# A long convolution over a period of 23040 in place of 25088: 91 frequencies along n1 in place of 99

## The chip, the cores and the metric

The kernel runs on one core of one Trainium2 chip. The metric is the device time of one execution in microseconds (us). A core has five engines that work side by side: PE (TensorE, matrix products), DVE (VectorE), ACT (ScalarE), POOL (GpSimd) and SP (SyncE, which here only issues DMAs). They meet at semaphores. Operands lie in the on-chip memory SBUF; PE writes into PSUM only.

## The reference

```python
S, D = 12480, 128                                # x, v: (1, S, D)
h = np.maximum(pos_emb @ w1, 0.0) @ w2           # (S, 64) -> (S, 64) -> (S, D)
h = h * np.exp(-0.01 * np.arange(S, dtype=np.float32))[:, None]
u = x * v
L = 2 * S
y = np.fft.irfft(np.fft.rfft(u, n=L, axis=1) * np.fft.rfft(h, n=L, axis=0)[None], n=L, axis=1)[:, :S]
x1 = (x * y)[0]                                  # (S, D)
a = x1 @ moe_w_in                                # (S, 2048)
x2 = (a * np.clip(a + 3.0, 0.0, 6.0) / 6.0) @ moe_w_out
b = x2 @ moe2_w_in
out = np.where(b > 0.0, b, np.exp(np.minimum(b, 0.0)) - 1.0) @ moe2_w_out
```

A causal convolution of each of 128 channels with a filter as long as the sequence, a product with x, and two gated layers with 2048 hidden columns. All in float32; the four large weight matrices arrive as float64 bit patterns. The convolution need not be taken over 2S points: any period will do at which the wrapped part of the full result falls outside the first S outputs, or is zero.

## The kernel before

**Transform.** The period is L = N1 x N2 = 196 x 128 = 25088. Position n is split as n1 x 128 + n2. Of the N1 rows only H1 = 98 hold data, and because the data are real NK = 99 frequencies k1 (0 to 98) are kept. The stages:

- *Filter* (`filter_hidden`): the hidden layer of the filter in 8 pieces, with the decay window.
- *First transform* (`first`, L308): for every n2, over n1, for 4 channels at a time: 8 matmuls, each with 2 x NK columns of the table `t1`. Done for the channels of u (`first_u`, into `au`) and for the hidden filter columns (`first_r`, into `Ar`). ACT copies the result out of PSUM (L311). `au` lies as [channel, k1, re/im], so one channel's row is 2 x NK floats.
- *Signals* (`signal`, L264 to L267): POOL multiplies x by v for 4 channels and folds the halves (three operations, on 98 partitions). There are 16 per half of the channels. They don't depend on NK.
- *Second transform* (`second_all`): for every k1, over n2, with one 128 x 128 table `gm` per k1. The k1 go in *groups* of 4 (`KGROUPS`), the last groups are smaller. In half 0 of the channels PE transforms the filter rows too (`second_r`, L333, copied back by ACT at L336), then the signal (`second_u`, L325) and the filter's output layer (`second_h`, L340) into one PSUM tile `z`. Then the complex product (`second`): ACT copies the filter part to `ta` (L345), DVE makes two products `tb` and `tc` (L347), POOL adds and subtracts them into `au` (L353, two operations a group). In half 0 two groups, A and B, go together: a *pair*. Half 1 takes the groups one by one and doesn't transform the filter again.
- *Middle*: between the two halves, `first_u` of half 1 (L308) alternates with the *third transform* (`third`, L362) of half 0, over 128 columns of `cs`; DVE combines the results (L368).
- *Third transform* of half 1, then the *fourth* (L479, over k1, 97 or 98 columns), the product with x (L525), and the two gated layers (L594 and L638), each split into high and low parts.

**Weights.** The float64 weights are converted beside the convolution. `weight_steps` is a generator with 32 conversions of three steps:

- step 1: DVE L180, L181;
- step 2: ACT L184, L185 (these need L180), DVE L186, and DMAs: one store of the conversion before (L170, from ACT's queue) and one load (L165, from SP's);
- step 3: DVE L190 (needs L185), L191.

**Order.** Each engine executes in program order. `convert(n)` adds n to `due` and takes as many steps as are due. It is called behind every first transform of the first stage (rate `RATE[0]`), behind every group of half 0 (`RATE[1]`), every chunk of the middle (`RATE[2]`) and every group of half 1 (`RATE[3]`); in the halves only for groups with k0 below `KLAST`. The call stands at the end of a group, so its DVE and ACT operations stand ahead of the next group's copies and products:

```python
            for z, gm, k0, nk in g:
                if not early:
                    second_h(hf, z, k0, nk)
                second(hf, z, k0, nk)
                if hf == 0:
                    load_gm0(n + len(gms))
                n += 1
                convert(RATE[2 * hf + 1] if k0 < KLAST else 0)
```

PSUM holds four tiles of the pool `ps`. The table pieces of half 0 go through eight buffers (`gms`), those of half 1 through four (`ld`). `AHEAD` places two signals of half 1 between groups of half 0, `TAIL` marks where the filter rows of the last groups are transformed in one go. All loads are issued by SP in program order.

Of the kernel before, what the change touches and what calls it, by code (L numbers as in the profile page):

```python
# [16 lines left out]
PSUM = bass.MemoryType.PSUM  # L17

S, D, FO, FF = 12480, 128, 64, 2048
N1, N2 = 196, 128  # L20
L = N1 * N2
H1 = N1 // 2
NK = H1 + 1
HN = N2 // 2
NM = HN + 1
SP = H1 * N2
HP = H1 * HN
HD = D // 2
SHIFT = H1 // 4
TT = 512  # L30
# [6 lines left out]
LAG, DELAY = 5, 13  # L37
EX = 8
SIG = (16, 40)
KLAST = 72  # L40

# [1 line left out]
TOKENS = {  # L45
    (m, sg): (np.arange(H1) * N2 + m - 1 if sg else np.arange(H1 - 2, -1, -1) * N2 + N2 - 1 - m) for m, sg in CLASSES
}
# [4 lines left out]
def tables():  # L52
    n1, k1, k2 = np.arange(H1), np.arange(NK), np.arange(N2)
    i, m, a = np.arange(HN), np.arange(NM), np.arange(H1) - 2 * SHIFT - 1
    w = 2 * np.pi * (np.outer(n1 - SHIFT, k1) % N1) / N1
    c, s = np.cos(w), np.sin(w)

    t1 = np.stack([np.stack([c, -s], axis=2), np.stack([-s, -c], axis=2)], axis=1)
    k = k1[:, None] + N1 * k2
    w = np.pi * (((2 * i + 1)[:, None, None] * k) % (2 * L)) / L  # L60
    gm = np.concatenate([np.cos(w), np.sin(w)], axis=0)

    w = 2 * np.pi * (np.outer(k2, m) % N2) / N2
    c, s = np.cos(w), np.sin(w)
    cs = np.stack([
        np.concatenate([c[:, :HN], s[:, 1:HN], c[:, HN:]], axis=1),
        np.concatenate([c[:, :1], s[:, 1:HN], c[:, 1:]], axis=1),
    ], axis=1)
    w = 2 * np.pi * (np.outer(k1, a) % N1) / N1
    pa = np.stack([np.cos(w), -np.sin(w), np.sin(w), np.cos(w)], axis=1)  # L70
    ends = (m == 0) | (m == HN)
    w = 2 * np.pi * np.outer(k1, m) / L - np.where(ends, np.pi / 4, 0.0)
    c = np.outer(np.where((k1 == 0) | (k1 == H1), 1.0, 2.0) / L, np.where(ends, np.sqrt(0.5), 1.0))
    pm = np.stack([np.cos(w), np.sin(w)], axis=2) * c[:, :, None]
    win = folded(np.exp(-0.01 * np.arange(S, dtype=np.float32))[:, None])[:, 0].transpose(0, 2, 1)
    return [np.ascontiguousarray(z, dtype=np.float32) for z in (t1, gm, cs, pa, pm, win)]


def folded(z):

    z = np.pad(z, ((0, SP - S), (0, 0))).reshape(H1, N2, -1)
    return np.stack([z[:, HN:], z[:, HN - 1::-1]], axis=1).transpose(0, 3, 1, 2)
# [3 lines left out]
def tile_kernel(ctx, tc, xc, vc, xT, posT, w1_d, w2_d, moe_w, t1_d, gm_d, cs_d, pa_d, pm_d, win_d, outT):  # L86
# [15 lines left out]
    DS = HD + EX  # L102
    au = sctx.enter_context(tc.tile_pool(name="aup", bufs=1, side="right")).tile([128, 2 * NK * DS], F32, name="au")
    const = sctx.enter_context(tc.tile_pool(name="const", bufs=1, side="right"))
# [7 lines left out]
    QW = 2 * N2 * HD  # L112
    RW = 2 * NK * FO
    qb = big.tile([128, max(2 * QW, QW + RW + VW + 3 * VT + 2 * D)], F32, name="qb")

    Au = au.rearrange("p (d k r) -> p d k r", r=2, k=NK)
    Ar = qb[:, QW:QW + RW].rearrange("p (k f r) -> p f k r", f=FO, r=2)
    Rk = qb[:, QW:QW + RW].rearrange("p (k c) -> p k c", k=NK)
    Q = qb[:, :2 * QW].rearrange("p (h g d t) -> p h g d t", h=2, d=HD, t=2)
# [20 lines left out]
    def load_pos(n):  # L140
        for c in (slice(a * H1, b * H1) for a, b in list(zip(edges, edges[1:]))[n]):
            nc.sync.dma_start(pos_t[:, c], posT[:, c])

    load_pos(slice(0, 3))
    t1 = const.tile([H1, 2, 2 * NK], F32, name="t1")
    nc.scalar.dma_start(t1.rearrange("p f k -> p (f k)"), t1_d)
# [46 lines left out]
        store(len(jobs) - 1)  # L193

    weights = weight_steps()
    RATE = (1.1, 1.5, 1.5, 0.6)

    due = [0.0]

    def convert(n):  # L200
        due[0] += n
        while due[0] >= 1:
            due[0] -= 1
            next(weights, None)


    DC, KC, LOOK = 4, 4, 3
# [9 lines left out]
    def load_gm0(n):  # L217
        if n < len(KGROUPS):
            k0, nk = KGROUPS[n]
            nc.sync.dma_start(gms[n % len(gms)][:, :nk], gm_d[:, k0:k0 + nk])  # L220

    def load_u(n):
        xt = tile_of(lds, "ld", [H1, DC, 2, HN], 4)
        nc.sync.dma_start(xt, xc[:, n * DC:(n + 1) * DC])
        return n, xt

    def load_gm(k0, nk):
        gm = tile_of(lds, "ld", [128, KC, N2], 4)
        nc.sync.dma_start(gm[:, :nk], gm_d[:, k0:k0 + nk])
        return gm  # L230
# [10 lines left out]
    def groups(sizes):  # L241
        return list(zip(np.cumsum([0] + sizes[:-1]).tolist(), sizes))

    KGROUPS = groups([KC] * 22 + [3, 3, 2, 2, 1])

    AHEAD, TAIL = 7, 23
    for k in [*range(2 * NC), *KGROUPS]:
        loads.append(lambda k=k: load_gm(*k) if isinstance(k, tuple) else load_u(k))
    taken = [0]
# [5 lines left out]
    def take():  # L255
        ahead(taken[0] + 1 + LOOK)
        taken[0] += 1
        t, ready[taken[0] - 1] = ready[taken[0] - 1], None
        return t

    def signal(n, xt):
        if n:
            load_v(n + 2)
        nc.gpsimd.tensor_tensor(out=xt, in0=xt, in1=vts[n % 3], op=ALU.mult)  # L264
        ut = uts[n // NC][n % len(uts[n // NC])]
        nc.gpsimd.tensor_tensor(out=ut[:, :, 0], in0=xt[:, :, 0], in1=xt[:, :, 1], op=ALU.add)  # L266
        nc.gpsimd.tensor_tensor(out=ut[:, :, 1], in0=xt[:, :, 0], in1=xt[:, :, 1], op=ALU.subtract)  # L267
        return ut
# [58 lines left out]
    def second_r(n, count):  # L327
        r = ps.tile([128, 2 * KC, N2], F32, tag="ps", name="r")
        k0 = KGROUPS[n][0]
        for i in range(n, n + count):  # L330
            for j in range(KGROUPS[i][1]):
                k = KGROUPS[i][0] + j
                nc.tensor.matmul(r[:, k - k0], lhsT=Rk[:, k], rhs=gms[i % len(gms)][:, j], start=True, stop=True)  # L333
# [51 lines left out]
    def second_all(hf):  # L385
        n = 0

        def size(n):
            return min(2 if n == 0 or hf == 0 and n != TAIL - 1 else 1, len(KGROUPS) - n)

        def rows(n):
            if hf == 0 and n <= TAIL:
                second_r(n, size(n) if n < TAIL else len(KGROUPS) - TAIL)

        rows(0)
        while n < len(KGROUPS):
            if hf == 0 and n == len(KGROUPS) - AHEAD:
                for _ in range(EX // DC):
                    us.append(signal(*take()))

            rows(n + size(n))
            g = [
                (ps.tile([128, 2, KC, 2 * HD], F32, tag="ps", name="z"), take() if hf else gms[(n + i) % len(gms)], *k)
                for i, k in enumerate(KGROUPS[n:n + size(n)])
            ]

            early = hf == 1 and n == 0
            if early:
# [3 lines that stand above are left out]
                second_u(hf, z, gm, k0, nk)  # L412
# [9 lines that stand above are left out]
# [4 lines left out]
    for n, (kind, c) in enumerate(steps):  # L426
# [6 lines left out]
        if n < 2 * len(gms) and n % 2:  # L433
            load_gm0(n // 2)
        convert(RATE[0])
    second_all(0)
    emptied = groups([4] * 14)
    for c in range(NC):
# [4 lines left out]
        if c + EX // DC < NC:  # L443
            us.append(signal(*take()))
        convert(RATE[2])
    assert not emptied
# [264 lines left out]
```

## Time and profile before

| | |
|---|---|
| median of 3 runs | 1427.43 us (1424.81 to 1430.37) |
| profiled execution | 1427.71 us, span 1425.8 us |
| PE busy | 1395.5 us (98%) |
| DVE busy | 1206.4 us (85%) |
| ACT busy | 1010.9 us (71%) |
| POOL busy | 519.1 us (36%) |
| DMA | 60.71 MB, mean 43 GB/s |

The span is the time from the first to the last recorded instruction of the profiled execution. Busy shares are means over the whole span, in which the convolution is the first quarter and the gated layers the rest. A matmul in float32 shows as two records ("x16" is eight matmuls). An entry "[1.38 <-ACT ta L345]" says that the engine was idle for 1.38 us before this instruction, and which instruction ended the wait. The durations of consecutive instructions on an engine overlap slightly; the time from start to start is what one costs.

### The profile page before, as it was taken

To read this page: it belongs to the slowest core of one execution; us is meant where nothing else is said; L and a number is where in the kernel's file an instruction comes from. 1 tells how busy PE (TensorE), PEld (TensorE's weight loads), DVE (VectorE), ACT (ScalarE), POOL (GpSimd) and SP (SyncE) were. 2 spreads that over 40 slices of the span, in tenths; PEclk is the share of its full clock that TensorE was granted. 3 is DMA by queue.
4 is the path that set the end of the run, shared out by engine and by line. 5 is a ranking of instruction groups with operands and counts; after the bars stand their busy time and mean duration, and the time that the engine had idled before them with its cause. 6 is when DMAs were issued, how large, how long until landed. Compare 5 with 4: busy or idle time off the path is not lost.

```text
span 1425.8 us, 21334 instructions
## 1 busy us (share of the span) xinstructions
PE 1395.5 (98%) x8222; PEld 1176.6 (83%) x8222; DVE 1206.4 (85%) x1305; ACT 1010.9 (71%) x1196; POOL 519.1 (36%) x430
## 2 busy tenths in 40 slices
PE   7998899999999999999999999999999999999999
PEld 6788789998878888888888888888888888888887
DVE  7867688788899888888888888888888888888987
ACT  1754453356888877788877787777787778887776
POOL 6846988311332323232223232323222323222223
PEclk9999999999999999999999999999999999999999
DMA  6944356145000000000000000000000000000000
GB/s 205 257 149 131 93 170 171 38 116 171 1 0 8 8 8 8 0 8 9 8 8 0 8 9 8 8 3 6 8 8 8 8 1 8 8 8 9 1 8 18
DMA packets 36513, 60.71 MB, mean 43 GB/s; under 512 B 4274, under 2 KB 14780, under 8 KB 36284
## 3 DMA queue, kind: packets, MB, share of 16 engines
q1 hardware_dynamic: 31292, 54.68, 12.8%
q10 hardware_dynamic: 5120, 4.66, 1.0%
q8 instruction: 65, 1.06, 0.3%
q14 instruction: 36, 0.29, 0.1%
HBM read 48.74 MB, written 10.58 MB: 42 GB/s over the span
## 4 chain that ended last, share of the span: by engine, by line
PE 86%; DVE 4%; POOL 3%; DMA 3%; issue 2%; ACT 2%; SPq 0%; DVEq 0%; POOLq 0%; ACTq 0%
PE o L638 37%; PE h L594 37%; PE q L362 4%; PE pa L308 3%; PE y L479 2%; POOL au L353 1%; PE z L325 1%; PE z L340 1%; DVE tb L347 1%; DVE gs L628 1%; DVE tc L347 1%; POOL ld L264 1%; DMA qb<-in_vc 1%; ACT qb L336 1%; DMA xt<-in_xT 1%
## 5 line engine op out<-in xcount | busy, mean ns | idle before, releaser
L638 PE MATMUL o<-gs,w 128*128 128x512 f32 (+1 forms) x2400 | 574.9, 388 | 0.0
L607 POOL TENSOR_SCALAR a<-a 128x1024 f32<-128x1024 f32 (+1 forms) x200 | 292.9, 1464 | 731.4 <-ACT a L606 689.6
L638 PEld LDWEIGHTS o<-gs,w 128*128 128x128 f32 x2400 | 443.7, 188 | 96.8 <-ACT y L567 0.4
L628 DVE TENSOR_TENSOR gs<-g,gs 128x1024 fp32r<-128x1024 f32 (+1 forms) x400 | 484.5, 1211 | 8.4 <-ACT gs L623 8.4
L623 ACT CAST gs<-g 128x1024 fp32r<-128x1024 f32 (+1 forms) x400 | 408.8, 1024 | 55.9 <-DVE g L615 53.7
L615 DVE SCALAR_TENSOR_TENSOR g<-a,h 128x1024 f32<-128x1024 f32 (+1 forms) x200 | 238.8, 1194 | 131.1 <-ACT a L604 131.1
L594 PE MATMUL h<-xs,w 128*128 128x512 f32 (+1 forms) x1200 | 303.9, 389 | 3.2 <-POOL w L508 2.0
L594 PE MATMUL h<-x,w 128*128 128x512 f32 (+1 forms) x1200 | 299.0, 385 | 0.1
L606 ACT ACTIVATE a<-h 128x1024 f32<-128x1024 f32 (+1 forms) x200 | 201.2, 1006 | 95.2 <-PE h L594 93.7
L594 PEld LDWEIGHTS h<-xs,w 128*128 128x128 f32 x1200 | 222.9, 188 | 53.3 <-POOL w L508 2.4
L604 ACT ACTIVATE a<-h,three 128x1024 f32<-128x1024 f32 (+1 forms) x200 | 219.0, 1095 | 62.5 <-PE h L594 62.2
L594 PEld LDWEIGHTS h<-x,w 128*128 128x128 f32 x1200 | 222.3, 188 | 46.4 <-DVE g L617 0.9
L617 DVE SCALAR_TENSOR_TENSOR g<-a,h 128x1024 f32<-128x1024 f32 (+1 forms) x200 | 237.4, 1187 | 0.0
L353 POOL TENSOR_TENSOR au<-tb,tc 128x256 f32<-128x256 f32 (+3 forms) x108 | 91.0, 877 | 44.0 <-DVE tc L347 42.1
L347 DVE TENSOR_TENSOR tb<-z,ta 128x512 f32<-128x512 f32 (+3 forms) x54 | 34.7, 643 | 36.9 <-ACT ta L345 23.7
L508 POOL TENSOR_TENSOR w<-w 128x512 fp32r<-128x512 f32 x16 | 25.0, 1565 | 106.8 <-ACT w L507 106.8
L362 PEld LDWEIGHTS q<-cs,au 128*99 128x99 f32 x512 | 56.6, 170 | 5.5 <-issue 4.9
L362 PE MATMUL q<-cs,au 128*99 128x128 f32 x512 | 59.8, 275 | 1.2 <-DVE tc L347 1.0
L345 ACT COPY ta<-z 128x512 f32<-128x512 f32 (+3 forms) x54 | 28.9, 553 | 40.8 <-DVE tc L347 17.8
L308 PE MATMUL pa<-t,qb 98*64 98x198 f32 x512 | 50.2, 349 | 5.4 <-POOL qb L266 3.3
L368 DVE TENSOR_TENSOR qb<-q,tb 99x512 f32<-99x512 f32 (+2 forms) x68 | 41.4, 654 | 14.1 <-ACT tb L366 13.8
L308 PEld LDWEIGHTS pa<-t,qb 98*64 98x64 f32 x512 | 38.4, 144 | 17.0 <-POOL qb L267 4.5
(58 smaller groups left out, 976.1 us busy)
## 6 DMA issues: line engine op xcount, KB each, us to landing
ld<-in_xc SPq DMA_DIRECT2D x32, 196.0 KB
qb<-in_vc SPq DMA_DIRECT2D x32, 196.0 KB
out_T<-y SPq DMA_DIRECT2D x24, 256.0 KB
xt<-in_xT SPq DMA_DIRECT2D x31, 195.0 KB
qb<-in_mw SPq DMA_DIRECT2D x22, 256.0 KB
qb<-in_gm SPq DMA_DIRECT2D x22, 256.0 KB
ld<-in_gm SPq DMA_DIRECT2D x22, 256.0 KB
w_scratch<-qb ACTq DMA_DIRECT2D x32, 128.0 KB
```

The source lines that it names most:

```text
L308: nc.tensor.matmul(pa[f * HN:(f + 1) * HN, j, :2 * NK], lhsT=src(j, f), rhs=t1[:, f], start=True, stop=True)
L353: nc.gpsimd.tensor_tensor(out=Au[:, slots(hf), k0:k0 + nk, r], in0=m1[:, :, :nk, r], in1=m2[:, :, :nk, 1 - r], op=op)
L362: nc.tensor.matmul(q[:NK, r, j], lhsT=Au[:, s0 + j, :, r], rhs=cs[:, r * N2:(r + 1) * N2], start=True, stop=True)
L594: nc.tensor.matmul(h[:, j], lhsT=wslice(2 * m - 2, a, 2 * u + j), rhs=x[:, b], start=i == 0, stop=i == 2)
L604: nc.scalar.activation(a, h, AF.Relu, bias=three)
L606: nc.scalar.activation(a, h, AF.Exp)
L607: nc.gpsimd.tensor_scalar(a, a, 1.0, 0.0, op0=ALU.min, op1=ALU.max)
L615: nc.vector.scalar_tensor_tensor(g, a, 6.0, h, op0=ALU.min, op1=ALU.mult)
L617: nc.vector.scalar_tensor_tensor(g, a, -1.0, h, op0=ALU.add, op1=ALU.max)
L623: nc.scalar.copy(t[:, 0], g)
L628: nc.vector.tensor_tensor(out=t[:, 1], in0=g, in1=t[:, 0].bitcast(F32), op=ALU.subtract)
L638: nc.tensor.matmul(o[:, :WID[t]], lhsT=wslice(2 * m - 1, a, 2 * u + j), rhs=gs[:, b, j], start=u == 0 and j == 0 and i == 0, stop=u == NU ...
```

## The change

The decay window `exp(-0.01 n)` underflows to zero in float32 from n = 10398 on, so the filter has 10398 taps, and a period of 12480 + 10398 - 1 = 22877 is enough. N1 becomes 180, L = 23040, NK = 91. H1, the number of rows with data, stays 98 and is now worked out from S. The groups become 20 of 4, then 3, 3, 2, 2, 1 (22 of 4 before). The rates, the last converting group and the place of the tail follow.

```diff
-N1, N2 = 196, 128
+
+ZERO = 10398
+N1, N2 = 180, 128
 L = N1 * N2
-H1 = N1 // 2
-NK = H1 + 1
+H1 = -(-S // N2)
+NK = N1 // 2 + 1
+assert L >= S + ZERO - 1
...
-KLAST = 72
+KLAST = 64
...
-    c = np.outer(np.where((k1 == 0) | (k1 == H1), 1.0, 2.0) / L, np.where(ends, np.sqrt(0.5), 1.0))
+    c = np.outer(np.where((k1 == 0) | (k1 == N1 // 2), 1.0, 2.0) / L, np.where(ends, np.sqrt(0.5), 1.0))
...
-    RATE = (1.1, 1.5, 1.5, 0.6)
+    RATE = (1.1, 1.6, 1.6, 0.7)
...
-    KGROUPS = groups([KC] * 22 + [3, 3, 2, 2, 1])
+    KGROUPS = groups([KC] * 20 + [3, 3, 2, 2, 1])
 
-    AHEAD, TAIL = 7, 23
+    AHEAD, TAIL = 7, 21
```

Lines of the changed kernel below the table code are numbered 5 higher: its L185, L186 are step 1, L191 (with ACT's L189, L190) step 2, L195, L196 step 3, L352 the products.

DVE in half 0, the second pair of groups, before: `tb`, `tc` of group A, then step 3 of one conversion, `tb`, `tc` of group B, then steps 1 and 2 of the next.

```order
L347 TENSOR_TENSOR tb<-z,ta 128x4x64x2
L347 TENSOR_TENSOR tc<-z,ta 128x4x64x2
L190 SCALAR_TENSOR_TENSOR qb<-qb 128x256
L191 SCALAR_TENSOR_TENSOR qb<-qb 128x256
L347 TENSOR_TENSOR tb<-z,ta 128x4x64x2
L347 TENSOR_TENSOR tc<-z,ta 128x4x64x2
L180 TENSOR_SCALAR qb<-qb 128x256
L181 TENSOR_SCALAR qb<-qb 128x256
L186 SCALAR_TENSOR_TENSOR qb<-qb 128x256
```

The same pair on DVE in the changed kernel:

```order
L352 TENSOR_TENSOR tb<-z,ta 128x4x64x2
L352 TENSOR_TENSOR tc<-z,ta 128x4x64x2
L195 SCALAR_TENSOR_TENSOR qb<-qb 128x256
L196 SCALAR_TENSOR_TENSOR qb<-qb 128x256
L185 TENSOR_SCALAR qb<-qb 128x256
L186 TENSOR_SCALAR qb<-qb 128x256
L352 TENSOR_TENSOR tb<-z,ta 128x4x64x2
L352 TENSOR_TENSOR tc<-z,ta 128x4x64x2
L191 SCALAR_TENSOR_TENSOR qb<-qb 128x256
```

Step 1 has moved from behind group B's products to ahead of them. All nine converting pairs before have the order of the first listing. Of the eight in the changed kernel the first pair has it too; pairs 1 and 2 have the second one; pair 3 has steps 3 and 1 behind A, 2 and 3 behind B; pairs 4 and 5 have 1 behind A, 2 and 3 behind B; pairs 6 and 7 have 1 and 2 behind A and 3 behind B.

ACT in half 0 of the changed kernel, around pair 6: the copy of the filter rows (L341), the copy `ta` of group A (L350), the conversion's two operations and its store, and the copy `ta` of group B.

```order
L341 COPY qb<-r 128x1024
L350 COPY ta<-z 128x512
L189 ACTIVATE qb<-qb,ramps 128x256
L190 ACTIVATE qb<-qb,ramps 128x256
L175 DMA w_scratch<-qb 128x256
L350 COPY ta<-z 128x512
```

Before, both copies of every pair stand together ("COPY ta<-z 128x512 x2"), ahead of the conversion's operations; in pairs 6 and 7 they now stand on either side of them.

## Rows read from the trace of the kernel before

**Rows 1.** Seven stages: length; busy PE, PEld, DVE, ACT, POOL; PE clock; DMA share; GB/s.

```profile
27.30:85.40 58.10, 55.26 (x558) 44.40 (x559) 43.69 (x62) 38.26 (x58) 42.66 (x42) 0.94 0.77 219
85.40:144.60 59.20, 52.65 (x444) 50.85 (x444) 46.19 (x81) 26.20 (x46) 34.67 (x36) 1.00 0.43 137
144.60:159.60 15.00, 11.52 (x92) 10.94 (x91) 7.20 (x13) 4.70 (x10) 13.39 (x17) 0.91 0.18 54
159.60:212.40 52.80, 52.80 (x482) 43.49 (x482) 43.35 (x73) 27.11 (x46) 50.05 (x50) 0.96 0.49 149
212.40:263.50 51.10, 49.16 (x429) 48.46 (x429) 41.23 (x72) 19.78 (x37) 43.56 (x54) 1.00 0.54 151
263.50:340.00 76.50, 74.48 (x1281) 73.68 (x1282) 64.09 (x139) 38.23 (x89) 4.14 (x4) 1.00 0.34 89
340.00:1425.80 1085.80, 1080.17 (x4800) 887.09 (x4798) 942.65 (x849) 854.58 (x912) 314.00 (x213) 1.00 0.03 10
```

**Rows 2.** Chain of waits from the start: start us, us, what; first pair of half 0.

```profile
85.38 0.69 DVE tb L347
```

**Rows 3.** Timeline, end of half 0's full pairs: start us, us, engine, line, op, out<-in, xcount.

```profile
144.62 0.69 DVE L347 TENSOR_TENSOR tb<-z,ta 128x512 f32<-128x512 f32 x1 [1.39 <-ACT ta L345]
...
146.06 3.27 POOL L353 TENSOR_TENSOR au<-tb,tc 128x256 f32<-128x256 f32 x4 [2.12 <-DVE tc L347]
```

**Rows 4.** Timeline of one pair in the middle of half 0.

```profile
98.54 0.69 DVE L347 TENSOR_TENSOR tb<-z,ta 128x512 f32<-128x512 f32 x1 [1.37 <-ACT ta L345]
...
99.74 0.42 DVE L190 SCALAR_TENSOR_TENSOR qb<-qb 128x256 int32<-128x256 int32 x1
...
99.97 1.16 PE L325 MATMUL z<-au,qb 128*128 128x128 f32 x8 [0.79 <-DVE tc L347]
...
100.97 1.95 PE L340 MATMUL z<-qb 128*128 128x128 f32 x16
101.07 0.68 DVE L347 TENSOR_TENSOR tb<-z,ta 128x512 f32<-128x512 f32 x1
...
102.27 0.28 DVE L180 TENSOR_SCALAR qb<-late 128x256 int32<-128x256 int32 x1
...
102.58 0.51 ACT L184 ACTIVATE qb<-qb,ramps 128x256 f32<-128x256 int32 x1 [3.66 <-DVE qb L180]
...
102.76 1.95 PE L333 MATMUL r<-qb 128*128 128x128 f32 x16
102.78 0.95 DVE L186 SCALAR_TENSOR_TENSOR qb<-late,qb 128x256 f32<-128x256 uint32 x1
...
103.54 0.99 ACT L336 COPY qb<-r 128x1024 f32<-128x1024 f32 x1
104.43 1.07 ACT L345 COPY ta<-z 128x512 f32<-128x512 f32 x2
...
105.12 0.69 DVE L347 TENSOR_TENSOR tb<-z,ta 128x512 f32<-128x512 f32 x1 [1.38 <-ACT ta L345]
```

**Rows 5.** Timeline, POOL, last operation of the last signal.

```profile
210.02 0.73 POOL L267 TENSOR_TENSOR late<-ld 98x256 f32<-98x256 f32 x1
```

**Rows 6.** Chain of waits in the middle stage: an early and the last first transforms.

```profile
168.10 1.49 PE pa L308 x16
...
209.12 3.24 PE pa L308 x32
```

**Rows 7.** Timeline of POOL in half 1.

```profile
231.19 8.84 POOL L353 TENSOR_TENSOR au<-tb,tc 128x256 f32<-128x256 f32 x10 [0.63 <-DVE tc L347]
240.65 8.85 POOL L353 TENSOR_TENSOR au<-tb,tc 128x256 f32<-128x256 f32 x10 [0.62 <-PE z L325]
```

**Rows 8.** Timeline of the middle stage: a signal's first operation alone and beside L191.

```profile
166.78 1.28 POOL L264 TENSOR_TENSOR ld<-ld,qb 98x512 f32<-98x512 f32 x1
...
169.50 2.06 POOL L264 TENSOR_TENSOR ld<-ld,qb 98x512 f32<-98x512 f32 x1
...
170.47 1.38 DVE L191 SCALAR_TENSOR_TENSOR qb<-qb 128x256 f32<-128x256 f32 x1
```

More of the change, by code (lines that the diff above doesn't have):

```diff
@@ L72, in tables @@
     w = 2 * np.pi * np.outer(k1, m) / L - np.where(ends, np.pi / 4, 0.0)
-    c = np.outer(np.where((k1 == 0) | (k1 == H1), 1.0, 2.0) / L, np.where(ends, np.sqrt(0.5), 1.0))
+    c = np.outer(np.where((k1 == 0) | (k1 == N1 // 2), 1.0, 2.0) / L, np.where(ends, np.sqrt(0.5), 1.0))
     pm = np.stack([np.cos(w), np.sin(w)], axis=2) * c[:, :, None]
-    win = folded(np.exp(-0.01 * np.arange(S, dtype=np.float32))[:, None])[:, 0].transpose(0, 2, 1)
+    window = np.exp(-0.01 * np.arange(S, dtype=np.float32))
+    assert not window[ZERO:].any()
+    win = folded(window[:, None])[:, 0].transpose(0, 2, 1)
     return [np.ascontiguousarray(z, dtype=np.float32) for z in (t1, gm, cs, pa, pm, win)]
```

## The prediction

> **What bounds the kernel now.** I read the table of stages first, because the span is a row of stages with different limits. The stretch from 340.00 us on (the two gated layers) is 1085.80 us long and PE is busy for 1080.17 of it [rows 1]; no number of that part depends on the period, so it only starts earlier. The same holds for 263.50 to 340.00, the third transforms of half 1 and the fourth transform: their matmuls stream 128 columns of `cs`, or 98 positions, as often as before; only the count of weight columns or rows falls from 99 to 91. Everything that can be won lies before 263.50.
>
> There the limit changes from stage to stage. In 85.40 to 144.60 (second transform, half 0) no engine is full: PE 52.65, DVE 46.19, ACT 26.20, POOL 34.67 of 59.20 us [rows 1]. So I read the chain of waits there, and it shows a loop: the first `tb` product of the first pair of groups starts at 85.38 [rows 2], that of the tenth at 144.62 [rows 3]: nine steps of 59.24 / 9 = 6.58 us. The timeline of one pair [rows 4] shows what closes the loop. DVE works without a gap from `tb` at 98.54 to the end of L186 at 102.78 + 0.95 = 103.73, that is 5.19 us, then idles 1.38 us for ACT's copy `ta`. That copy is late because ACT executes in order: L184, ahead of it, waited 3.66 us for DVE's L180, which stands at the end of the pair. From the end of L180 (102.27 + 0.28 = 102.55) it is L184, L185, the copy of `r` (L336), the copy `ta` (L345), and only then the next `tb` at 105.12: 2.57 us, of which DVE can fill no more than its L181 and L186. So **the period is set by where step 1 of a conversion stands among DVE's products**, not by the amount of work.
>
> From 146.06 to 210.75 POOL is the chain: it starts when the first product of the tenth pair is there [rows 3] and ends with L267 at 210.02 + 0.73 [rows 5]; it is busy 13.39 of 15.00 us, with 1.46 of the missing 1.61 ahead of that start, and 50.05 of 52.80 [rows 1]. PE looks full between 159.60 and 212.40, but the last two first transforms take 3.24 us [rows 6] where one takes 1.49 [rows 6]: 0.26 us more than two, a sign of waiting for the last signal from POOL. In 212.40 to 263.50 POOL is again the slowest: ten `au` operations (five groups) in 8.84 us, and the next ten start 9.46 us after them [rows 7], with one gap of 0.62 us per conversion.
>
> **The change part by part.** Durations are of the profiled execution, 1427.71 us (span 1425.80).
>
> *1. Half 0 loses one pair.* 99 frequencies were 11 full pairs of groups and a tail; 91 are 10 and the same tail. A pair costs one period: 6.58 us.
>
> *2. The new rate moves the conversion steps within the pairs.* Nine pairs took three steps each, always with step 3 behind group A and steps 1, 2 behind group B (first listing of the change). With 1.6 per group, eight pairs take 25 steps, and the phase drifts. I price each kind from [rows 4]: `tb` and `tc` 1.20 us from start to start of what follows (98.54 to 99.74), step 3 1.33 (99.74 to 101.07), step 1 0.51 (102.27 to 102.78), step 2's DVE part 0.95.
> - Pair 0 keeps the old order: 6.58.
> - Pairs 1 and 2 (A: 3, 1; B: 2): L180 ends 1.20 + 1.33 + 0.28 = 2.81 behind the pair's start; ACT's chain of 2.57 runs beside the products of B. Period 5.38; DVE alone would need 5.19.
> - Pair 3 (A: 3, 1; B: 2, 3) has a fourth step: 5.19 + 1.33 = 6.52.
> - Pairs 4 and 5 (A: 1; B: 2, 3): ACT is ready at 1.48 + 2.57 = 4.05, so DVE sets it: 5.19.
> - Pairs 6 and 7 (A: 1, 2; B: 3): ACT converts ahead of B's copy `ta` (second listing). L184 starts at 1.51, L336 could follow 0.96 later (102.58 to 103.54), so B's copy starts at 2.47 and its product at 3.16 (0.69 from copy to product, 104.43 to 105.12), 0.50 later than DVE is free (1.20 + 0.51 + 0.95 = 2.66): 5.69.
>
> Pairs 1 to 7 together: 2 x 5.38 + 6.52 + 2 x 5.19 + 2 x 5.69 = 39.04 us, where seven old periods are 46.06. **Gain 7.0 us.** What is late next? PE. Its pair is twice 1.0 (L325, 99.97 to 100.97) and twice 1.79 (L340, 100.97 to 102.76, and as many passes of L333), that is 5.6 us, or 39.1 for seven: level with DVE. PE now runs almost a pair ahead (L340 of the next pair is finished at 102.92, 1.51 us before the copy that needs it), so I charge nothing. If it sets the pace, the tail starts up to 1.5 us later; and POOL's chain, which has slack against PE there, would still start from the tenth (now ninth) pair's product. Each pair loads two tables and one weight piece as before; at 5.6 us a pair the 137 GB/s of this stretch become 137 x 6.58 / 5.6 = 161, well under the 219 of the stage before [rows 1].
>
> *3. The tail of half 0 and the middle stage (144.60 to 212.40).* The tail has the same groups and the same two signals. In the middle PE saves 16 of 198 columns in 256 passes: 1.49 us / 16 = 93 ns a pass, times 16/198 = 7.5 ns, 1.9 us in all. But POOL's signals don't depend on the period, and they are the chain, so I count zero. The bounds: a gain of 1.9 if PE were the limit after all; on the other side a loss, because 25 or 26 steps instead of 24 stand in this stage. A POOL L264 takes 1.28 us by itself and 2.06 beside DVE's L191, which itself takes 1.38 there [rows 8]; 24 steps hold 16 such DVE operations, 26 hold 17 or 18: one or two collisions of 0.78 us, a loss of up to 1.6.
> The Trainium skill (page "SBUF — State Buffer", section "Who interferes with whom") says that a VectorE instruction with two SBUF inputs and a GpSimd instruction that reads SBUF block each other, the later one until the earlier is done. The trace agrees in the pair just named, and by that rule the middle would be slower by 0.8 to 1.6 us instead of level.
>
> *4. Half 1 (212.40 to 263.50)* loses two full groups. POOL's two groups are 4 x 0.884 = 3.5 us (8.84 / 10, [rows 7]). The rate 0.7 for 16 groups makes 11 steps where 0.6 for 18 made 10 or 11: the gaps of 0.62 stay four. PE would save two groups of about the same (0.9 of L340 and 1.0 of L325 each, by [rows 4]), so nothing appears behind it. **Gain 3.5.** Bounds: 2.4 if DVE with its two products (1.20 a group) became the limit, 3.8 with the gaps (2 x 9.46 / 5).
>
> *5. First stage (to 85.40).* Here too PE's first transforms are 8% shorter, but transfers and POOL's signals end the waits; 125 passes lie on the chain before the transfers take over, at 7.5 ns: 0 to 0.9, I take 0.2. The rate there is not touched.
>
> Sum: 6.58 + 7.0 + 0 + 3.5 + 0.2 = **17.3 us**. 1427.71 - 17.3 = 1410.4; the median of the three runs is 0.28 us below the profiled execution, so **1410 us**. Between the ends: parts 3, 4 and 5 give 1408 to 1413, part 2 with PE as the limit 1412.
>
> **The rivals.**
> *The pairs don't get shorter.* The loop could be held at 6.58 us by something that the old order hides, such as PE's four PSUM buffers, a table that lands late, or a POOL operation. Then only one pair goes: 6.58 + 3.5 + 0.2 = 10.3, 1417. For it: PE waits inside each pair today. Against it: DVE's 1.38 us of idle time and ACT's 3.66 us both name one cause, and the change removes it. A mixture, where half of the 7.0 us comes, gives 1414.
> *The middle follows PE.* If POOL is not the chain between 159.60 and 210.75, 1.9 us more are won: 1408.
> *The new row distance costs time, and the kernel is slower.* `au` holds all frequencies of a channel in a row, 198 floats before and 182 now. POOL writes it with that step, PE reads it with that step. About 60 of POOL's `au` operations lie on the path (tail and half 1). The change loses when each takes more than 17.3 / 60 = 0.29 us longer, that is 1.17 in place of 0.884 us; at 1.3 us the time would be 1435. Nothing in the trace shows a dependence on this step, and both layouts touch two floats and jump; but no row excludes it.
> *The change removes less than it says.* The listing of the changed order shows the 16 groups with steps, so this is left out.
>
> **How the numbers follow.** Shorter pairs, with the middle level or PE-bound: 0.68. Pairs only partly shorter or not at all: 0.27. A new cost that eats the gain or more: 0.05, of which 0.02 end slower. The three runs before differ by 5.6 us, so a median can move by two. The range takes the first two cases with that: 1405 to 1418.5. About 0.5%, 7.1 us, is what a measurement of this kernel tells from no change; faster than 1420.3 is 0.92, within 0.06, slower 0.02.
>
> **What would show it.** In the new trace the `tb` starts of half 0 should stand at steps of 6.58, then 5.4, 5.4, 6.5, 5.2, 5.2, 5.7, 5.7, with no DVE wait of 1.38 us for `ta` in pairs 2 to 6; the tenth pair's place (now the ninth's) near 131 instead of 144.62; POOL's `au` and signals from there without a gap for about 64.7 us; half 1 near 47.6 us instead of 51.1; and the rest, from the third transforms of half 1 on, as long as before. The prediction is wrong if the steps stay at 6.58, if the middle takes over two microseconds more, or if the stretch behind 263.50 changes its length at all.

## The result, and the profile after

The changed kernel takes **1409.01 us** (median of 5 runs, 1407.2 to 1411.62), the kernel before 1427.43 (1424.81 to 1430.37): the ratio is 0.9868, with a 95% interval of 0.9851 to 0.9885. A second comparison gave 0.9902 (0.9879 to 0.9924). The prediction was 1410, between 1405 and 1418.5. The sum came out within 0.1 us of the profiled difference, but three of its terms did not come out, and they made up for each other: that is luck.

Both spans cut at the same events: the first `tb` of half 0, the first `tb` behind the converting pairs, the first and the third first transform of the middle, the end of the last one, the first matmul of the long run of third transforms of half 1, and the first matmul of the gated layers behind their start-up. The columns are those of [rows 1]. Before:

```profile
85.38:144.62 59.24, 52.69 (x445) 50.89 (x444) 46.21 (x81) 26.23 (x46) 34.67 (x36) 1.00 0.43 137
144.62:159.62 15.00, 11.52 (x92) 10.94 (x92) 7.22 (x13) 4.70 (x10) 13.41 (x17) 0.91 0.18 54
159.62:168.10 8.48, 8.48 (x66) 6.86 (x68) 5.99 (x13) 3.43 (x7) 8.35 (x12) 0.76 0.09 22
168.10:212.36 44.26, 44.26 (x418) 36.57 (x417) 37.31 (x61) 23.65 (x38) 41.68 (x38) 1.00 0.56 173
212.36:263.47 51.11, 49.17 (x428) 48.47 (x428) 41.25 (x73) 19.75 (x37) 43.53 (x54) 1.00 0.54 151
263.47:347.43 83.96, 79.95 (x1304) 77.77 (x1304) 68.19 (x143) 44.06 (x96) 6.14 (x5) 1.00 0.39 104
347.43:1425.80 1078.37, 1074.73 (x4776) 883.03 (x4776) 938.54 (x846) 848.77 (x906) 312.04 (x212) 1.00 0.02 8
```

After:

```profile
85.13:132.95 47.82, 45.92 (x400) 45.14 (x399) 43.30 (x74) 24.53 (x42) 29.16 (x32) 1.00 0.50 150
132.95:147.47 14.52, 10.04 (x87) 9.66 (x86) 7.10 (x13) 3.61 (x8) 13.74 (x17) 0.98 0.24 74
147.47:156.79 9.32, 9.32 (x66) 8.17 (x68) 7.56 (x15) 3.63 (x7) 9.16 (x14) 0.67 0.10 29
156.79:199.06 42.27, 42.27 (x418) 36.23 (x417) 38.23 (x59) 23.79 (x40) 37.68 (x38) 1.00 0.60 182
199.06:247.13 48.07, 45.83 (x396) 44.96 (x396) 40.30 (x73) 18.51 (x35) 39.85 (x50) 1.00 0.51 149
247.13:330.29 83.16, 79.93 (x1305) 77.76 (x1305) 67.52 (x143) 44.00 (x96) 6.13 (x5) 1.00 0.38 104
330.29:1408.40 1078.11, 1074.75 (x4776) 883.14 (x4776) 938.44 (x846) 848.44 (x906) 311.75 (x212) 1.00 0.02 8
```

| stretch | before | after | difference | predicted |
|---|---|---|---|---|
| start to the first `tb` of half 0 | 85.38 | 85.13 | -0.25 | -0.2 |
| converting pairs (9, then 8) | 59.24 | 47.82 | -11.42 | -13.6 |
| tail of half 0 | 15.00 | 14.52 | -0.48 | 0 |
| middle | 52.74 | 51.59 | -1.15 | 0 |
| half 1 | 51.11 | 48.07 | -3.04 | -3.5 |
| third and fourth transform, start of the layers | 83.96 | 83.16 | -0.80 | 0 |
| gated layers | 1078.37 | 1078.11 | -0.26 | 0 |
| span | 1425.80 | 1408.40 | -17.40 | -17.3 |

The gated layers are untouched, as they should be; PE is full in both. Two thirds of the gain lie in the stretch of the pairs. The timeline of DVE there, after the change (the counterpart of [rows 3, 4]; each `tb` shown opens a pair):

```profile
85.13 0.69 DVE L352 TENSOR_TENSOR tb<-z,ta 128x512 f32<-128x512 f32 x1 [6.92 <-ACT ta L350]
...
91.71 0.69 DVE L352 TENSOR_TENSOR tb<-z,ta 128x512 f32<-128x512 f32 x1 [1.38 <-ACT ta L350]
...
94.35 0.82 DVE L185 TENSOR_SCALAR qb<-qb 128x256 int32<-128x256 int32 x1
...
97.74 0.69 DVE L352 TENSOR_TENSOR tb<-z,ta 128x512 f32<-128x512 f32 x1 [0.84 <-ACT ta L350]
...
103.77 0.69 DVE L352 TENSOR_TENSOR tb<-z,ta 128x512 f32<-128x512 f32 x1 [0.84 <-ACT ta L350]
...
110.87 0.68 DVE L352 TENSOR_TENSOR tb<-z,ta 128x512 f32<-128x512 f32 x1
...
113.67 0.69 DVE L191 SCALAR_TENSOR_TENSOR qb<-qb 128x256 f32<-128x256 uint32 x1
114.28 1.07 DVE L195 SCALAR_TENSOR_TENSOR qb<-qb 128x256 int32<-128x256 int32 x1
...
116.25 0.68 DVE L352 TENSOR_TENSOR tb<-z,ta 128x512 f32<-128x512 f32 x1
...
121.62 0.68 DVE L352 TENSOR_TENSOR tb<-z,ta 128x512 f32<-128x512 f32 x1
...
127.28 0.68 DVE L352 TENSOR_TENSOR tb<-z,ta 128x512 f32<-128x512 f32 x1
...
132.95 0.68 DVE L352 TENSOR_TENSOR tb<-z,ta 128x512 f32<-128x512 f32 x1
```

The starts stand 6.58, 6.03, 6.03, 7.10, 5.38, 5.37, 5.66 and 5.67 us apart, where the old ones stood 6.58 apart throughout. The wait for `ta` (1.38 us in every pair before) is 1.38 behind the unchanged pair 0, 0.84 behind pairs 1 and 2 and nothing behind the others; in pairs 6 and 7 DVE waits 0.46 and 0.47 us for group B's copy instead. L185 at 94.35 takes 0.82 us, and its counterpart L180 took 0.28 in its old place [rows 4]; L195 at 114.28 takes 1.07 where L190 took 0.42.

POOL's first operation behind the pairs and the end of its last signal (the counterpart of [rows 3, 5]):

```profile
134.37 3.27 POOL L358 TENSOR_TENSOR au<-tb,tc 128x256 f32<-128x256 f32 x4 [0.62 <-DVE tc L352]
...
194.51 0.91 POOL L272 TENSOR_TENSOR late<-ld 98x256 f32<-98x256 f32 x1
```

From 134.37 to 195.42 it needs 61.05 us; before, from 146.06 to 210.75, it needed 64.69. The last first transform ends 3.64 us behind the end of the last signal (195.42 to 199.06), where it ended 1.61 behind it before (210.75 to 212.36).

### The profile page after: what moved, and what is told of

The parts are those of the page before. It is cut to its first block, busy times and chain, and to the rows that moved or that the text cites. A ratio compares the mean times of both kernels' runs of the same rounds, so it can differ in the third digit from the quotient of the medians.

```text
span 1408.4 us, 21132 instructions
## 1 busy us (share of the span) xinstructions
PE 1380.4 (98%) x8142; PEld 1167.4 (83%) x8142; DVE 1205.6 (86%) x1297; ACT 1005.2 (71%) x1191; POOL 506.2 (36%) x422
## 4 chain that ended last, share of the span: by engine, by line
PE 85%; DVE 6%; POOL 3%; DMA 3%; issue 2%; ACT 1%; SPq 0%; DVEq 0%; POOLq 0%; ACTq 0%
PE o L643 37%; PE h L599 37%; PE q L367 4%; PE y L484 2%; PE pa L313 2%; POOL au L358 2%; DVE gs L633 1%; PE z L345 1%; PE z L330 1%; DVE tc L352 1%; DVE qb L288 1%; PE r L338 1%; DVE tb L352 1%; DMA xt<-in_xT 1%; POOL ld L269 1%
## 5 line engine op out<-in xcount | busy, mean ns | idle before, releaser
L358 POOL TENSOR_TENSOR au<-tb,tc 128x256 f32<-128x256 f32 (+3 forms) x100 | 82.5, 857 | 39.8 <-DVE tc L352 38.5
L367 PE MATMUL q<-cs,au 128*91 128x128 f32 x512 | 60.2, 276 | 1.2 <-DVE tc L352 1.0
L367 PEld LDWEIGHTS q<-cs,au 128*91 128x91 f32 x512 | 56.9, 164 | 5.4 <-issue 3.7
L313 PE MATMUL pa<-t,qb 98*64 98x182 f32 x512 | 47.6, 336 | 8.5 <-POOL qb L271 4.7
L352 DVE TENSOR_TENSOR tb<-z,ta 128x512 f32<-128x512 f32 (+3 forms) x50 | 31.9, 637 | 26.1 <-POOL au L358 13.4
L350 ACT COPY ta<-z 128x512 f32<-128x512 f32 (+3 forms) x50 | 26.9, 547 | 36.4 <-DVE tc L352 24.3
L373 DVE TENSOR_TENSOR qb<-q,tb 91x512 f32<-91x512 f32 (+2 forms) x68 | 41.2, 649 | 10.1 <-ACT tb L371 9.9
```

The lines of the kernel that those rows point to most:

```text
L313: nc.tensor.matmul(pa[f * HN:(f + 1) * HN, j, :2 * NK], lhsT=src(j, f), rhs=t1[:, f], start=True, stop=True)
L358: nc.gpsimd.tensor_tensor(out=Au[:, slots(hf), k0:k0 + nk, r], in0=m1[:, :, :nk, r], in1=m2[:, :, :nk, 1 - r], op=op)
L367: nc.tensor.matmul(q[:NK, r, j], lhsT=Au[:, s0 + j, :, r], rhs=cs[:, r * N2:(r + 1) * N2], start=True, stop=True)
```

## The experiments

All are built from the kernel before or from the changed one. For stretches, the profiled executions are compared at the events of the table above; lines of the changed kernel are numbered 5 higher.

### The old order with 91 frequencies

```diff
-    RATE = (1.1, 1.6, 1.6, 0.7)
+    RATE = (1.1, 1.5, 1.6, 0.7)
```

> 91 frequencies with the conversion steps of half 0 kept in the old order (step 3 behind group A, steps 1 and 2 behind B in all eight pairs). Theory, the order sets the period: the tb starts of half 0 stand at steps of 6.58 us throughout, eight pairs take 52.6 us where the changed kernel took 47.8, and the time is 4.8 us above the changed kernel's, near 1414. Rival, the pairs got shorter because of the 91 frequencies themselves (layout, fewer bytes): 47.8 us and 1409, whatever the order.

Measured: 1417.92 us (1415.92 to 1419.52; 0.9932 of the kernel before, 0.9915 to 0.995). DVE's timeline, two pairs:

```profile
92.36 0.69 DVE L352 TENSOR_TENSOR tb<-z,ta 128x512 f32<-128x512 f32 x1 [1.39 <-ACT ta L350]
...
98.95 0.69 DVE L352 TENSOR_TENSOR tb<-z,ta 128x512 f32<-128x512 f32 x1 [1.39 <-ACT ta L350]
```

The step is 6.58 or 6.59 in all eight pairs, 52.67 us in all, and the 1.39 us of waiting for `ta` are back. The time is 8.9 us above the changed kernel's instead of the expected 4.8. In the profiled executions the difference is 5.7, of which 4.85 lie in the pairs and 0.65 ahead of them, in the start, whose spread is shown further down. The medians were not taken side by side; where they were, further down, they differ by 2.9.

### Another order with 91 frequencies

```diff
-    RATE = (1.1, 1.6, 1.6, 0.7)
+    RATE = (1.1, 1.5, 1.6, 0.7)
...
+    convert(1)
     second_all(0)
```

> 91 frequencies, one conversion step taken ahead of half 0 and rate 1.5, so that all eight pairs have step 1 behind group A and steps 2 and 3 behind B. Theory: every step of the tb starts is near 5.4 us, as in pairs 4 and 5 of the changed kernel; eight pairs take 43 to 44.6 us (the latter if PE with 5.58 us a pair sets the pace), 3 to 5 us less than the changed kernel, so 1404 to 1406. Rival (the order does not matter): 1409.

Measured: 1405.37 us (1403.24 to 1413.28; 0.9851, 0.9819 to 0.9882). DVE's timeline, two pairs; L185, step 1, stands behind group A's products:

```profile
100.56 0.69 DVE L352 TENSOR_TENSOR tb<-z,ta 128x512 f32<-128x512 f32 x1
...
101.77 0.28 DVE L185 TENSOR_SCALAR qb<-qb 128x256 int32<-128x256 int32 x1
...
105.97 0.69 DVE L352 TENSOR_TENSOR tb<-z,ta 128x512 f32<-128x512 f32 x1
...
111.37 0.69 DVE L352 TENSOR_TENSOR tb<-z,ta 128x512 f32<-128x512 f32 x1
```

Seven steps of 5.40 or 5.41 and a first one of 5.47, 43.29 us for eight pairs. The theory's numbers held. This order is 3.6 us below the changed kernel, with intervals that overlap; the runs side by side further down confirm that it is the faster one.

### The same two edits with 99 frequencies

Both kernels here are the kernel before with one edit: first the step ahead of half 0, then, in the second listing, the rate 1.6.

```diff
+    convert(1)
     second_all(0)
```

> The kernel before (99 frequencies), with one conversion step taken ahead of half 0, so that all nine converting pairs have step 1 behind A, 2 and 3 behind B. Theory: nine pairs take 48.4 to 50.2 us in place of 59.24, a gain of 9 to 11 us without any change of the period: 1417 to 1418.5. Rival (the shorter pairs came with the 91 frequencies): no change, 1427.

Measured: 1419.89 us (1417.79 to 1420.16; 0.9939, 0.9923 to 0.9955). The first `tb`, the second pair's, and the one behind the ninth pair:

```profile
86.98 0.69 DVE L347 TENSOR_TENSOR tb<-z,ta 128x512 f32<-128x512 f32 x1 [4.42 <-ACT ta L345]
...
92.45 0.69 DVE L347 TENSOR_TENSOR tb<-z,ta 128x512 f32<-128x512 f32 x1
...
135.66 0.69 DVE L347 TENSOR_TENSOR tb<-z,ta 128x512 f32<-128x512 f32 x1
```

Nine pairs take 48.68 us in place of 59.24: 10.56 us of gain with the period as it was. The total lies 1.4 to 2.9 us above the expected one. The profiled execution took 1417.79, as expected, although its first `tb` came at 86.98 instead of 85.38; the rest of the way differs by less than a microsecond. What made the other three runs 2 us longer no profile shows.

```diff
-    RATE = (1.1, 1.5, 1.5, 0.6)
+    RATE = (1.1, 1.6, 1.5, 0.6)
```

> The kernel before (99 frequencies), with the rate of half 0 alone set to 1.6. Theory: the nine converting pairs take steps of about 6.6, 6.0, 6.0, 7.1, 5.4, 5.4, 5.7, 5.7 and 6 us, some 54 us in place of 59.24, a gain near 5 us, 1422. Rival: no change, 1427; what the changed kernel won would then be all due to the frequencies.

Measured: 1419.75 us (1414.79 to 1425.16; 0.9947, 0.9929 to 0.9964). The steps are 6.59, 6.05, 6.05, 7.10, 5.40, 5.39, 5.67, 5.67 and 6.73, 54.65 us: the rate alone gives the same steps with 99 frequencies as with 91, so the layout and the number of frequencies have no part in them. The last step had been expected at 6 us. The runs are spread over 10 us, and the profiled one is the slowest of them, with its first `tb` at 89.02, so the total says little here. The rate alone is worth 4.6 us in the pairs, and 1.2 us more in half 1 (49.92 instead of 51.11), where fewer steps are left to do.

### What holds up step 1: POOL's sums left out

```diff
-        for r, op in ((0, ALU.subtract), (1, ALU.add)):
+        for r, op in ((0, ALU.subtract), (1, ALU.add)) if hf or k0 >= KLAST else ():
```

> The changed kernel without POOL's two sums of the complex product in the 16 converting groups of half 0 (so their results are left out). Theory: the steps of pairs 1 to 3 came out 0.6 us longer than predicted because POOL's operation of the same pair holds up DVE's L185 (0.82 in place of 0.28 us), and those of pairs 4 and 5 because PE needs 5.40 us a pair. Without POOL's sums L185 takes 0.28 us everywhere and the steps are 6.58, then 5.4 to 5.5, 5.4 to 5.5, 6.5, 5.4, 5.4, 5.7, 5.7. Rival: L185 is slow there for a reason of DVE's or ACT's own; then it stays at 0.8 us and the steps at 6.03, 6.03, 7.10.

Measured: one run, 1405.44 us. L185 in pairs 1 and 3, and L196 in pair 3:

```profile
94.70 0.29 DVE L185 TENSOR_SCALAR qb<-qb 128x256 int32<-128x256 int32 x1
...
104.46 0.42 DVE L196 SCALAR_TENSOR_TENSOR qb<-qb 128x256 f32<-128x256 f32 x1
104.92 0.29 DVE L185 TENSOR_SCALAR qb<-qb 128x256 int32<-128x256 int32 x1
```

It takes 0.29 us instead of 0.82, so POOL's operation of the same pair was what held it up. The Trainium skill (page "SBUF — State Buffer", section "Who interferes with whom") says that VectorE's `tensor_scalar` can run in a mode that takes the port shared with GpSimd, and that the later of the two then waits. The trace agrees: L185 is such an instruction, 0.28 or 0.29 us without POOL and 0.82 beside it. The operations with two SBUF inputs became shorter too: L196 from 0.95 to 0.42 us in every pair, L195 from 1.07 to 0.42 behind L191 in pair 3, L191 from 0.95 to 0.43 in pair 0 (in pairs 1 to 3 it had taken 0.41 already). The same section of the Trainium skill says that such instructions contend with a GpSimd instruction that reads SBUF, which POOL's sums do; the trace agrees.

The steps are not those expected: 5.98, 4.92, 5.31 and then 5.40 to the end. I had only taken L185 to be slowed, and with L191 and L196 short as well DVE is no longer near the pace. The chain of waits shows what is, from pair 3 on:

```profile
104.83 1.83 PE z L330 x16
106.67 1.79 PE z L345 x16
108.45 1.79 PE r L338 x16
110.24 1.83 PE z L330 x16
```

PE, 1.84 + 1.78 + 1.79 = 5.41 us for the 48 records of a pair, without a gap. That is the floor of a pair, and the order of `p91_y` runs at it: from its third pair to its eighth PE is busy for all of the 32.42 us, and DVE for 32.22. Pairs 4 and 5 of the changed kernel are another matter, although they took 5.38 and 5.37 us: there DVE is busy for 10.68 of 10.75 us and PE for 10.13, so DVE with its lengthened steps set the pace, and not PE, as I had expected.

### Does the middle follow PE or POOL?

```diff
-    t1 = const.tile([H1, 2, 2 * NK], F32, name="t1")
-    nc.scalar.dma_start(t1.rearrange("p f k -> p (f k)"), t1_d)
+    t1 = const.tile([H1, 4 * NK + 16], F32, name="t1")
+    nc.vector.memset(t1[:, 4 * NK:], 0.0)
+    nc.scalar.dma_start(t1[:, :4 * NK], t1_d)
...
-                    pa[f * HN:(f + 1) * HN, j, :2 * NK], lhsT=src(j, f), rhs=t1[:, f], start=True, stop=True
+                    pa[f * HN:(f + 1) * HN, j, :2 * NK + 16], lhsT=src(j, f), rhs=t1[:, 2 * NK * f:2 * NK * f + 2 * NK + 16],
+                    start=True, stop=True
```

> The changed kernel with the first transforms streaming 198 columns again (16 of no use); everything else as in the changed kernel. Theory: the middle stage follows PE, so its 16 chunks take 0.1 us longer each and the stretch from its first to its last first transform is 1.6 to 1.9 us longer (51.6 becomes 53.2 to 53.5). Rival: POOL's signals set the middle; then the stretch stays within 0.3 us.

Measured: one run, 1412.36 us. The chain of waits: the first two first transforms of the middle together, the third, and the last two.

```profile
151.09 4.81 PE pa L314 x32
...
159.56 1.49 PE pa L314 x16
...
200.48 2.83 PE pa L314 x32
```

The same of the changed kernel (before: [rows 6]):

```profile
147.47 5.12 PE pa L313 x32
...
156.79 1.38 PE pa L313 x16
...
196.44 2.62 PE pa L313 x32
```

From the third first transform on, the 198 columns take 200.48 + 2.83 - 159.56 = 43.75 us and the 182 take 196.44 + 2.62 - 156.79 = 42.27: 1.48 us from 14 chunks, 0.106 each (1.49 against 1.38 a chunk). So this part follows PE. The chain of waits of the kernel before runs along PE there too, without a gap, from 159.62 to the end of the stage; two of its rows:

```profile
169.59 1.93 PE q L362 x16
171.52 1.49 PE pa L308 x16
```

It needed 44.26 us with the same 198 columns; 0.41 of the remaining 0.5 is the last pair of first transforms (3.24 against 2.83), the wait for POOL that had been read in [rows 6].
The whole middle grew by only 0.63 us, not 1.6 to 1.9, because its first two transforms and the products behind them took 8.47 us here and 9.32 in the changed kernel. That isn't their columns: it is PE's clock. In that stretch it is granted 0.76 here (8.47 us), 0.76 before (8.48 us) and 0.67 after (9.32 us), and 1.00 from then on: in the changed kernel 0.50, the lower of the two levels (1.2 GHz), from 146.83 to 153.66, and then the upper one (2.4 GHz). PE had stood idle shortly ahead for 4.08, 3.30 and 4.07 us, so the length of that idle time alone does not say how much of the stretch runs at the lower level.

### The distance of au's rows

```diff
-    au = sctx.enter_context(tc.tile_pool(name="aup", bufs=1, side="right")).tile([128, 2 * NK * DS], F32, name="au")
+    au = sctx.enter_context(tc.tile_pool(name="aup", bufs=1, side="right")).tile([128, 2 * 99 * DS], F32, name="au")
...
-    Au = au.rearrange("p (d k r) -> p d k r", r=2, k=NK)
+    Au = au.rearrange("p (d k r) -> p d k r", r=2, k=99)[:, :, :NK]
```

> The changed kernel with the rows of au 198 floats apart again, of which 182 are used. Theory: the distance costs nothing; POOL's sums and PE's second transforms take the same mean times within 1%, half 0 and half 1 the same stretches (47.8 and 48.1 us). Rival: the new distance has a price, and with the old one POOL's sums are shorter than 0.857 us in the mean.

Measured: one run, 1408.85 us. POOL's sums, in the view of groups by line (xcount | busy us, mean ns):

```profile
L358 POOL TENSOR_TENSOR au<-tb,tc 128x256 f32<-128x256 f32 (+3 forms) x100 | 82.7, 864 | 39.6 <-DVE tc L352 37.7 <-PE z L330 1.9
```

864 ns against 857 in the changed kernel (861 in its second profile), 278.4 against 277.6 ns for a record of PE's second transforms, 47.90 us against 47.82 for the eight pairs and 48.1 us in both for half 1. The slower rival has nothing to it. One thing differs: from its third first transform on, the middle takes 43.14 us in place of 42.27, because one first transform in it lasts 2.28 us, held up by two conversion steps in a row on DVE (of their four operations L196 takes 1.38, L185 0.70 and L186 0.82 us beside POOL's signals). The same wait, 2.43 us, is in `p91_nopool`, which has the new row distance, so it does not come from the rows.

### Half 1's conversions moved to the middle

The kernel of `p91_y` with another pair of rates:

```diff
-    RATE = (1.1, 1.5, 1.6, 0.7)
+    RATE = (1.1, 1.5, 2.3, 0.0)
```

> The kernel with step 1 behind group A in all eight pairs (1405 us), and the eleven conversion steps of half 1 moved to the middle stage (rate 2.3 there, none in half 1). Theory: half 1 loses its four gaps of 0.63 us and runs at POOL's or PE's 1.77 to 1.81 us a group, 2.5 to 3 us shorter; the middle has 7 or 8 more collisions of DVE and POOL, and with POOL already busy nearly all the time there it becomes 2 to 5 us longer: 1404 to 1408, no gain beyond noise. Rival, the middle has room: 1402.5.

Measured: 1413.43 us (1411.1 to 1414.67; 0.9887, 0.9869 to 0.9905): a loss of 8 us against `p91_y`. Half 1 is 3.06 us shorter (45.74 against 48.80), as expected. The middle is 7.2 us longer (58.96 against 51.71), more than the 2 to 5 that collisions on POOL had been counted for. The chain of waits in the middle:

```profile
161.68 1.20 DVE qb L373 x2
162.88 0.62 DVE qb L191
163.49 1.42 DVE qb L195
...
165.69 1.27 DVE qb L373 x2
```

For most of the stage it runs along DVE now, from the third transform's sums (L373) through the conversion steps to the next sums; two transfers, of 3.80 and 3.62 us, stand on it as well. The steps are long because of the collisions: L186 lasts 1.36 us at 160.32 beside POOL's L269, 0.28 without. The count had charged them to POOL; they made DVE the limit. A further 4.3 us of the 8 lie ahead of half 0, in a stage that is the same in both.

### The three orders side by side

The changed kernel and the two other orders with 91 frequencies once more, side by side.

> The changed kernel itself, beside the two that follow, on one chip. Theory: 0.987 of the kernel before, as measured; its eight converting pairs take 47.8 us whenever it runs.

> 91 frequencies with the old order of the steps in half 0, side by side with the changed kernel. By the stretch of the eight pairs (52.7 and 47.8 us) it should be 4 to 6 us slower than the changed kernel; the runs on different chips showed 8.9. Should the difference stay near 9, something beyond the pairs depends on the order.

> 91 frequencies with step 1 behind group A in all eight pairs, side by side with the changed kernel. By the stretch of the pairs (43.3 and 47.8 us) it should be 4 to 5 us faster, near 0.984 of the kernel before. Rival: PE, which then runs without a gap in half 0, or the middle gives it back: equal within 1.5 us.

Measured, as ratios to the kernel before: old order 0.9928 (0.9906 to 0.9949), changed kernel 0.9902 (0.9879 to 0.9924), step 1 behind A 0.9863 (0.9842 to 0.9885); medians 1416.36, 1413.49 and 1406.93 us. The differences are 2.9 and 6.6 us, where the pairs make 4.8 and 4.5. The slowest run of the order with step 1 behind A (1409.35) is below the fastest of the changed kernel (1410.6). The eight pairs repeat to 0.1 us: 52.61, 47.83, 43.30. What doesn't repeat is the start: the first `tb` of half 0 came at 85.13 us in the first profile of the changed kernel and at 88.50 in this one. From there to the end the two executions take 1323.3 and 1322.6 us. Counted in this way, from the first `tb` of half 0 to the end of the span, the profiles of these orders read:

| | 99 frequencies | 91 frequencies |
|---|---|---|
| old order (steps of 6.58) | 1340.4 | 1328.4 and 1328.4 |
| rate 1.6 | 1334.4 | 1323.3 and 1322.6 |
| step 1 behind A | 1328.9 | 1319.6 and 1316.8 |

The 91 frequencies alone are worth 12 us in the old order, the rate 5 to 6 more. The two profiles of one kernel, 1319.6 and 1316.8, show what this way of counting still leaves open. 1.2 us of their difference lie in the middle (51.71 and 50.50), 1.6 in the gated layers (1078.2 and 1076.6), and PE's granted clock goes with both: up to the third first transform of the middle it is 0.66 in the first and 0.79 in the second, and at the start of the layers it falls to the lower level in the first and stays at 1.00 in the second, after 1.96 and 1.95 us of idle PE.

## Why the prediction was right, and where it was not

**The bound and its cause: right.** The loop in half 0 was put down to the place of step 1 among DVE's products. Putting it back (52.67 us for eight pairs) or elsewhere (43.29), with either number of frequencies, moves the period as the reading said. In the changed kernel the next `tb` of pair 1 comes 2.57 us behind the end of L185 (95.17 to 97.74), as it came 2.57 behind that of L180 before.

**Half 0 loses a pair: right.** With the old order eight pairs take 52.67 us and nine took 59.24: 6.57 for the predicted 6.58.

**The order within the pairs: right in kind, 2.2 us too much.** The step that failed is the price of pairs 1 to 5, where each operation was given its duration from its old place. Pairs 1 to 3 came out at 6.03, 6.03 and 7.10 for 5.38, 5.38 and 6.52: in its new place behind step 3, L185 meets POOL's sum of the same pair and takes 0.82 us. POOL's share was known in the prediction, but charged to the middle only. Pairs 4 and 5 came out at 5.38 and 5.37 for 5.19, again by durations from the old place: L195 meets POOL's sum there and step 3 takes 1.97 us for 1.33, while step 2 takes 0.61 for 0.95 and step 1 0.41 for 0.51. PE's floor is 5.41; the prediction had put it at 5.58, by two batches of L325 of 1.0 us each of which one had followed a wait. Pairs 6 and 7 (5.66 and 5.67 for 5.69) were right.

**The middle: wrong choice between the bounds.** "POOL's signals are the chain, so I count zero" was the step that failed; PE was busy for 52.80 of 52.80 us in [rows 1] and was the limit but for 0.4 us at the end; the 0.26 us that had been read as a sign of POOL's chain were a part of these and of nothing more. The steady part became 1.99 us shorter (44.26 to 42.27): 1.48 by the columns of 14 chunks, 0.41 by the wait that went, 0.1 by the third transforms between them (1.93 and 1.92 us each). The bound of 1.9 had only the columns in it, so that it fits so closely is chance. Of the 1.99, 0.84 went back at the start of the middle, where the granted clock was 0.67 in place of 0.76; in the second profile of the changed kernel, with 0.74 there, the whole middle takes 50.74 us. The feared extra collisions didn't show: in the changed kernel L269, the signal's first operation, takes 1.366 us in the mean of all 32, where L264 took 1.515. It takes 1.339 in `p99_y`, which differs from the kernel before by one step taken earlier: what decides is the phase of the steps, and not their number, by which the prediction had counted the collisions. In the case of [rows 8] L264, which began 0.97 us ahead of L191, took longer as well, so the rule quoted there, by which the later one waits, covers only half of it.

**Half 1: right, 0.5 us too much.** The gaps did not stay four. POOL in half 1 of the changed kernel (counterpart of [rows 7]):

```profile
216.60 7.18 POOL L358 TENSOR_TENSOR au<-tb,tc 128x256 f32<-128x256 f32 x8 [0.62 <-DVE tc L352]
224.41 7.18 POOL L358 TENSOR_TENSOR au<-tb,tc 128x256 f32<-128x256 f32 x8 [0.63 <-DVE tc L352]
```

Four groups, not five, lie between two gaps of 0.62, and there are five gaps in all: 2 x 1.77 - 0.62 = 2.9 us; measured 3.04.

**Not predicted:** 0.48 us less in the tail and 0.80 us less between the third transforms and the layers. Over the other kernels of this study the latter stretch takes 82.6 to 83.7 us with either number of frequencies, and the tail 14.5 to 15.0, so both are put down to spread and not to the change. The prediction had called any change behind 263.50 a sign of being wrong; measured is 1.06 us less there, and that sign was set too sharp for such a spread.

**The rivals.** The pairs that stay at 6.58 (1417) are what the old order gives: 1417.9 and 1416.4. The row distance costs nothing. The middle does follow PE: it became 1.15 us shorter in the first profile and 2.00 in the second.

## What to carry to other kernels

Where no engine is full and two in-order engines hand work to each other, look for the instruction that stands at the end of one engine's round and at the head of the other's: moving it was worth 18% of the stage here (59.24 to 48.68 us with 99 frequencies), with no work removed. When an instruction is moved, its duration moves too: price it beside what will run at the same moment on the engine that shares its port, not with its time from the old place. And compare stretches between events, since an early stage that waits for transfers can move the whole span by more than the effect one looks for.

## What the runs showed that I had not expected

The start is the largest source of spread: the first `tb` of half 0 came at 84.29 us in `p91_y` and at 88.60 in `p91_y_mid`, which differs from it only later, while the eight pairs of one order repeat within 0.1 us. What sets it was not tried; waits for transfers lie on that chain in all of them. And the same 32 records of first transforms at the start of the middle took 4.06 us in `p91_row` and 5.12 in the changed kernel, after 4.12 and 4.07 us of idle PE: the granted clock of the stretch up to the third first transform was 0.81 in the one and 0.67 in the other. The gated layers show the same: in four of the thirteen profiles PE's clock stays at 1.00 at their start and they take 1076.6 to 1077.0 us, in the other nine it falls and they take 1078.1 to 1078.4, with 1.95 to 1.99 us of idle PE ahead in every one.
